# A four-part recurrence with eight experts behind it: expert 6's result by rows, paced index casts, a first slice in halves

## The chip, the core and the metric

The kernel runs on one core of one Trainium2 chip. A core has five engines that work at the same time, each with a queue of its own: TensorE (PE, products of matrices, with a separate row PEld for loading weights), VectorE (DVE), ScalarE (ACT), GpSimd (POOL) and SyncE (SP, which only issues transfers); GpSimd issues transfers too. They meet through semaphores. The metric is the device time of one execution in microseconds (us); less is better. The clock of TensorE has two levels, 1.2 and 2.4 GHz, and the profile shows the granted one as a share of the full clock.

## The reference, cut to what matters

```python
# attention: a recurrence over seq = 768 for 4 x 8 heads of 48
for t in range(S):
    S_re, S_im = ar*S_re - ai*S_im + kv, ar*S_im + ai*S_re      # a_re, a_im normalised by min(mag, .999)/(mag + 1e-6)
    y[:, :, t] = np.einsum('bhd,bhde->bhe', q[:, :, t], S_re)
# 3072 tokens of 384 -> the expert of the largest logit, in the order of tokens, up to a capacity
logits = x @ w_gate;  expert_idx = np.argmax(logits, axis=1);  gate_w = probs[arange(N), expert_idx]
disp[e, counts[e]] = x[i]                                        # 8 experts
h = np.maximum(np.einsum('ecd,edf->ecf', disp, w1), 0.0)         # 384 -> 1024
y = np.einsum('ecf,efd->ecd', h, w2)                             # 1024 -> 384
out[i] = gate_w[i] * y[expert_idx[i], pos[i]]
```

## The kernel before

Attention is done in four groups of eight units (a unit is one batch's chunk of 96 tokens). For each group, slices of the decay factors are loaded, normalised (`norm`: a square on ScalarE, then logarithm, exponential and three VectorE steps per slice, L305 to L374) and multiplied up by a scan (`scan`: pairs of VectorE steps, L404 and L409, that go through the slice from its last position to its first). The scaled queries and keys go through a scratch tensor in HBM (`scr`) and come back turned. A unit then has transposes and products on TensorE (`tr` L629, `pa` L645, `y` L706 and L711), a mask on VectorE (`a_sb`, L649), a copy to `xt` on ScalarE (L900), the gate's product (L924), a turn back to tokens (L911) and a last copy on ScalarE (L917), with which the unit's 96 rows of x are complete.

Behind groups of units comes a routing round (`routing`; the table `CUTS` says after which chunk of which group): logits (L952), the choice of the expert (L960 to L965), counts (`pp`, L970, L975), slots (L983 to L986), the weight (L996 to L1006), one cast of the slot numbers to an index per chunk of 96 tokens (L1010, VectorE), and one scatter for each chunk (`send`, L1024, GpSimd), which writes 96 rows of x to `disp`, the tensor of the experts' rows in HBM. Seven transfers first fill `disp` (L853). The last three chunks are `LATE`: expert 0's rows are read from `disp` (`mload`, L1074, SP's queue) when all other chunks have been sent, and the three chunks' rows are added to them on TensorE (`mt`: L1094 turns what was read, L1088 adds a chunk through a 0/1 matrix `own`, L1084).

The second stage goes through the experts in turn in steps of 128 of the 1024 hidden columns: the first product (`ph`, L1220, nine products), its split into two parts (ScalarE L1266, VectorE L1267), and the second product two steps later. For experts 0 to 6 that is `second` (L1228), with tokens on the columns of the result; at the expert's end the result is copied (L1166 to L1168), turned (`yt`, L1174), scaled (L1184, VectorE) and scattered to the output (L1185, GpSimd). The last expert has `second_rows` (L1241), with tokens on the partitions of the result, which needs no copy and no turn.

All of the attention stage is ordered by a planner (`Plan`): each operation has an engine, a cost written by hand and a due time (`want`), worked out from `BEGIN`, the planned start of each group; the planner picks the operation that can start first and writes the order of each engine's queue. `apart` sets a least distance between the planned starts of two operations, here between one send and the next (`APART`, one number for each group). `fill_gaps` then puts products that nobody reads (`s_all` from `ident`, L226) into gaps of TensorE's plan that are over 0.4 us, from a planned time `begin` on. The queues run in this order; the planned times are not kept on the chip.

Of the kernel before, what the change touches and what calls it, by code (L numbers as in the profile page):

```python
# [172 lines left out]
def dve(n):  # L173
    return .068 + n * .00104


def act(n):
    return .045 + n * .00086


class Att:
# [95 lines left out]

    def norm(self, g, j, s0):

        nc, plan = self.nc, self.plan  # L280
# [25 lines left out]
        o = plan.op(K + ("xa",), "ACT", act(2 * n * D) + .1, xa, w, after=[K + ("load",)], bufs=[a_, a4_])  # L306
        if g == 0 and j < 1:
            def xb():
                x = self.a4[g, j][:, 0:n, 3, :]
                nc.vector.tensor_tensor(out=x, in0=st['sq'][:, 0], in1=st['sq'][:, 1], op=ALU.add)  # L310
                st[0] = x
            o = plan.op(None, "DVE", dve(n * D), xb, w, after=[o], bufs=[a4_])
            parts = [(0, n, o, a4_)]
        elif by_dma:
            def acc():
                nc.gpsimd.dma_start(out=st['flat'][:, 0], in_=st['flat'][:, 1], accum_op=ALU.add)
            o = plan.op(K + ("acc",), "POOL", .6, acc, w - 2, after=[o], bufs=[a4_], kb=24 * n, extra=3.)
            parts = [(0, n, o, a4_)]
        else:
            parts = self.sums_of(plan, K, lambda: (st['sq'][:, 0], st['sq'][:, 1]), n, [o], w, st, [a4_])  # L320
# [60 lines left out]
    def scan(self, g, j, wants):  # L381
# [3 lines left out]
        n = SIZES[j]  # L385
        a4_ = ("a4", g, j)
        for s in range(n - 1, -1, -1):
            if j == 0 and s == n - 1:
# [23 lines left out]
            before = [("s", g) + prev[1:]] if ("s", g) + prev[1:] in plan.names else []  # L412
            m = plan.op(None, "DVE", .27, None, want, after=before + [K + ("i",), K + ("r",)], bufs=bufs)
            a = plan.op(("s", g, j, s), "DVE", .169, None, want, after=[m], bufs=[a4_, xy_])
# [315 lines left out]
    def routing(self, b, c, w, span):  # L730
# [18 lines left out]
        for i in range(n):  # L749
            x = plan.op(None, "DVE", .12, fs['cast'][i], w + (5 + i) * s, after=[o])  # L750
            o_ = plan.op(K(("send", i)), "POOL", 1.0, fs['send'][i], w + (5 + i) * s, after=[x] + ([("mload",)] if (b, c + 1) in LATE else []), kb=148, extra=2.)
            if rt.scattered is not None:
                o_.apart = (rt.scattered, APART[b])
            rt.scattered = o_

# [5 lines left out]
NACC = 4  # L761
BEGIN = (13, 67, 135, 203, 271)
FIRST = 8
BEHIND = 6
APART = (5, 5, 2.6, 1)

# [18 lines left out]

CUTS = [(0, 8), (1, 8), (2, 8), (3, 5), (3, 6), (3, 7), (3, 8)]
LATE = CUTS[-3:]
# [249 lines left out]
class Moe:  # L1037
# [119 lines left out]
    def finish_ops(self, e, tail, py):  # L1157
# [20 lines left out]
        def send(t):  # L1178
            m = parts[t]
            pt = py[t] if e == E_ - 1 else turn(t)  # L1180
            if 'o' not in st:
                st['o'] = self.p_x.tile([128, NT, DM], F32, tag="o", name=f"o_{e}", bufs=1)
            o = st['o']
            nc.vector.tensor_scalar(out=o[:m, t], in0=pt[:m, :DM], scalar1=tail[:m, t, 0:1], scalar2=None, op0=ALU.mult)  # L1184
            ins = nc.gpsimd.indirect_dma_start(  # L1185
                out=self.out, out_offset=bass.IndirectOffsetOnAxis(ap=tail[:m, t, 1:2].bitcast(U32), axis=0),
                in_=o[:m, t, :], in_offset=None, bounds_check=N - 1, oob_is_err=False).ins
            for other in self.scatters:
                self.tc.declare_no_dep(ins, other, reason="rows of different tokens")
            self.scatters.append(ins)  # L1190
        return [evac] + [lambda t=t: send(t) for t in range(len(parts))]

    def run(self, order, perm, check):
# [42 lines left out]
        def second_rows(e, f, hh, hl, py, t):  # L1236

            hi, lo = (w[1] for w in self.w[e, f // self.PF])
            ts, m = slice(t * LP, t * LP + LAST[t]), LAST[t]
            for i, (a, r) in enumerate(((hh, hi), (hl, hi), (hh, lo))):  # L1240
                nc.tensor.matmul(out=py[t][:m, :DM], lhsT=a[:, ts], rhs=r[:, f % self.PF],  # L1241
                                 start=f == 0 and i == 0, stop=f == NF - 1 and i == 2)
        py = {}
        LP, LAST = tiles(WIDTH[-1])
        c_order = ExitStack()
        c_order.enter_context(self.tc.manual_schedule(engines=ALL))
        for s in range(E_ * NF):
# [21 lines left out]
            if f == 0:  # L1269
                py[e] = [self.ps.tile([128, 512], F32, tag=f"y{m}", name=f"my{m}_{e}") for m in range(len(LAST) if e == E_ - 1 else KT)]  # L1270
            queue.append((e, f, hh, hl, py[e]))
            if len(queue) > self.LAG and s < E_ * NF - 1:
                x = queue.pop(0)
                if x[0] < E_ - 1:
                    second(*x)
                else:
                    for t in range(len(LAST)):
                        second_rows(*x, t)
            for op in later.pop(s, []):
                op()  # L1280
        assert not later
        fin = self.finish_ops(e, rows[e]['tail'], py[e])
        for t in range(len(LAST)):
            for x in queue:
                second_rows(*x, t)
            fin[1 + t]()
# [179 lines left out]
def kernel(ctx, tc, q, k, v, a_re, a_im, w_gate, w1, w2, av, xv, cen, vp, out):  # L1466
# [5 lines left out]
    with ExitStack() as c_main, ExitStack() as c_att:  # L1472
# [20 lines left out]
        for r in range(E_ * T // 512):  # L1493
            plan.op(("fill", r), "POOL", .9, lambda r=r: box['fill'][r](), 9 + 3 * r, kb=772)
        order = plan.solve()
        plan.fill_gaps(att.keep)
        cut = max(i for i, o in enumerate(order) if o.idx < early) + 1
# [118 lines left out]
```

## Time and profile before

| what | value |
|---|---|
| median of 3 runs | 640.82 us (640.61 to 641.45) |
| the profiled execution | 641.58 us, span 639.9 us, mean granted clock 0.936 |
| TensorE busy | 561.8 us (88%) |
| VectorE busy | 458.9 us (72%) |
| ScalarE busy | 383.5 us (60%) |
| GpSimd busy | 212.9 us (33%) |

Busy time is an average over stages with different limits, so the rows further down go by stages. The profiled execution has its own time: its span is the time between the first and the last instruction in the trace, and 1.7 us lie around it.

### The profile page before, as it was taken

The numbers are of one execution on the slowest core, as the hardware profiler recorded it, in microseconds if no ns is written. First come the engines' busy times: TensorE is split into PE (matmuls) and PEld (weight loads), VectorE is DVE, ScalarE is ACT, GpSimd is POOL, SyncE is SP. The second block draws the span as 40 slices with busy tenths as digits, with TensorE's granted clock in tenths as the row PEclk, the third lists the DMA queues.
The fourth block names the chain that finished last, engine by engine and source line by source line (L and its number), as shares of the span: only waits on it lengthen the run. The fifth ranks groups of instructions, "written<-read, shape, count | busy, mean of one in ns | idle before, by whom it ended". The sixth has DMA issues, their size and how long they took to land.

```text
span 639.9 us, 13273 instructions
## 1 busy us (share of the span) xinstructions
PE 561.8 (88%) x4662; PEld 489.7 (77%) x4662; DVE 458.9 (72%) x1340; ACT 383.5 (60%) x1034; POOL 212.9 (33%) x293
## 2 busy tenths in 40 slices
PE   2364569998999989999896889999999999999994
PEld 1122258786887868888785877999999999999993
DVE  3899979999999998999763244546665655655651
ACT  6465689989998899977652421344445344444540
POOL 9532314524459925464525031002020202112012
PEclk9666679999999999999999779999999999999997
DMA  6985588968899787885997231364545454455311
GB/s 214 297 245 147 147 203 231 241 189 207 196 230 251 213 228 168 213 223 135 215 242 209 55 91 29 109 184 125 163 129 158 138 169 155 155 165 159 101 37 37
DMA packets 75629, 108.81 MB, mean 170 GB/s; under 512 B 11716, under 2 KB 65853, under 8 KB 75553
## 3 DMA queue, kind: packets, MB, share of 16 engines
q1 hardware_dynamic: 58192, 57.37, 33.3%
q0 software_dynamic: 17360, 50.50, 29.1%
q8 instruction: 39, 0.64, 0.4%
q14 instruction: 38, 0.30, 0.2%
HBM read 71.51 MB, written 32.47 MB: 163 GB/s over the span
## 4 chain that ended last, share of the span: by engine, by line
PE 55%; DVE 20%; DMA 10%; ACT 9%; issue 4%; POOL 1%; POOLq 0%; DVEq 0%; ACTq 0%; SPq 0%
PE ph L1220 17%; PE my L1228 15%; DVE xy L404 4%; DMA scr<-qko 3%; DVE a L409 3%; PE pa L645 3%; PE tr L629 2%; DMA raw<-in_moe_w_dram 2%; PE n L272 2%; PE my L1241 2%; DMA qkc<-scr 2%; DVE qko L452 2%; PE s_all L660 2%; PE y L706 2%; DMA a<-in_av_dram 2%
## 5 line engine op out<-in xcount | busy, mean ns | idle before, releaser
L1266 ACT ACTIVATE hh<-ph 128x448 fp32r<-128x448 f32 (+7 forms) x64 | 32.7, 511 | 92.1 <-PE ph L1220 81.8
L1267 DVE SCALAR_TENSOR_TENSOR hl<-ph,hh 128x448 fp32r<-128x448 f32 (+7 forms) x64 | 37.2, 581 | 60.4 <-ACT hh L1266 59.6
L1185 POOL DMA_INDIRECT out_dram<-o,xr x26 | 25.7, 987 | 162.8 <-DVE o L1184 159.5
L1130 DVE TENSOR_TENSOR lo<-raw,hi 128x384 fp32r<-128x384 f32 (+2 forms) x128 | 65.7, 553 | 9.8 <-ACT hi L1129 9.7
L272 PE MATMUL n<-a,ident 128*128 128x384 f32 x92 | 44.8, 622 | 28.7 <-ACT a L305 28.7
L1220 PE MATMUL ph<-xh,hi 128*128 128x448 f32 (+7 forms) x192 | 69.5, 362 | 0.0
L1220 PE MATMUL ph<-xh,lo 128*128 128x448 f32 (+7 forms) x192 | 66.5, 347 | 0.0
L404 DVE TENSOR_TENSOR xy<-a 128x192 f32<-128x192 f32 (+1 forms) x199 | 61.5, 322 | 1.3 <-ACT a L374 1.1
L1129 ACT CAST hi<-raw 128x384 fp32r<-128x384 f32 (+2 forms) x128 | 59.1, 512 | 2.8 <-DMA raw<-in_moe_w_dram 2.8
L673 POOL DMA_DIRECT2D z<-sx x56 | 47.4, 1003 | 39.8 <-PE pa L645 12.4
L629 PE MATMUL tr<-ident,qkc 81*96 81x81 f32 x512 | 53.8, 241 | 5.6 <-DMA qkc<-scr 2.6
L1228 PE MATMUL my<-hh,lo 128*128 128x448 f32 (+6 forms) x168 | 58.7, 349 | 0.0
L1228 PE MATMUL my<-hh,hi 128*128 128x448 f32 (+6 forms) x168 | 58.6, 349 | 0.0
L1228 PE MATMUL my<-hl,hi 128*128 128x448 f32 (+6 forms) x168 | 58.6, 349 | 0.0
L649 DVE TENSOR_TENSOR a_sb<-pa,mask 96x384 f32<-96x384 f32 x64 | 35.1, 552 | 32.1 <-PE pa L645 21.1
L1024 POOL DMA_INDIRECT disp<-x,idx x32 | 42.1, 1315 | 46.1 <-DVE lm L961 22.4
L645 PE MATMUL pa<-qT,kT 128*96 128x96 f32 x512 | 56.9, 256 | 0.5 <-issue 0.4
L629 PEld LDWEIGHTS tr<-ident,qkc 81*96 81x96 f32 x512 | 43.3, 130 | 13.3 <-issue 4.0
L645 PEld LDWEIGHTS pa<-qT,kT 128*96 128x96 f32 x512 | 51.2, 170 | 2.5 <-issue 1.6
L272 PEld LDWEIGHTS n<-a,ident 128*128 128x128 f32 x92 | 20.0, 237 | 42.8 <-ACT a L305 24.6
L272 PE MATMUL p<-qko,ident 128*128 128x384 f32 x80 | 37.4, 598 | 15.3 <-ACT qko L441 15.2
L409 DVE TENSOR_TENSOR a<-xy 128x96 f32<-128x96 f32 (+1 forms) x218 | 49.8, 240 | 0.4
(224 smaller groups left out, 1459.0 us busy)
## 6 DMA issues: line engine op xcount, KB each, us to landing
raw<-in_moe_w_dram SPq DMA_DIRECT2D x64, 384.0 KB
qkc<-scr SPq DMA_DIRECT2D x32, 480.0 KB
scr<-qko POOLq DMA_DIRECT2D x44, 192.0 KB
scr<-qko POOLq DMA_DIRECT2D x20, 384.0 KB
a<-in_av_dram POOLq DMA_DIRECT2D x18, 384.0 KB
qkin<-in_xv_dram POOLq DMA_DIRECT2D x18, 384.0 KB
disp<-fill POOLq DMA_DIRECT2D x7, 772.0 KB
v<-in_vp_dram SPq DMA_DIRECT2D x32, 144.0 KB
```

The source lines that it names most:

```text
L272: nc.tensor.matmul(out=pt[:, :m], lhsT=self.ident, rhs=t[:, h:h + m], start=i == 0, stop=i == 1)
L404: nc.vector.tensor_tensor(out=st['xy'][:, :, cs].rearrange("p (u z) d -> p u z d", u=2), in0=a4[:, s, :, cs].rearrange("p (u z) d -> p u z ...
L409: nc.vector.tensor_tensor(out=self.a4[g, j][:, s, 0:2, cs], in0=xy[:, 0:4:2, cs], in1=xy[:, 1:4:2, cs], op=ALU.add)
L629: nc.tensor.transpose(out=pt[:, h * C:h * C + NE], in_=qk[:NE, 4 * hh + h, z_ * C:z_ * C + C], identity=self.ident[:NE, :NE])
L645: nc.tensor.matmul(out=pa[:, h * C:h * C + C], lhsT=kT[:, 4 * hh + h], rhs=qT[:, 4 * hh + h], start=True, stop=True)
L673: nc.gpsimd.dma_start(out=zn[a.start:a.stop or C], in_=st['sx'][o], accum_op=ALU.add)
L1024: ins = nc.gpsimd.indirect_dma_start(out=self.disp, out_offset=bass.IndirectOffsetOnAxis(ap=idx[:, c:c + 1], axis=0), in_=self.row(b, c0 + ...
L1129: return (lambda: nc.scalar.copy(out=hi[i][:, s], in_=raw[i][:, s]), lambda: nc.vector.tensor_tensor(out=lo[i][:, s], in0=raw[i][:, s], in ...
L1130: lambda: nc.vector.tensor_tensor(out=lo[i][:, s], in0=raw[i][:, s], in1=hi[i][:, s].bitcast(F32), op=ALU.subtract))
L1220: nc.tensor.matmul(out=ph[:, :W], lhsT=a[:, k, fs], rhs=r[:, k, :W], start=i == 0, stop=i == len(parts) - 1)
L1228: nc.tensor.matmul(out=py[m][:, :W], lhsT=a[:, f % self.PF, ms], rhs=r[:, :W], start=f == 0 and i == 0, stop=f == NF - 1 and i == 2)
L1267: nc.vector.scalar_tensor_tensor(out=hl[:, :W], in0=ph[:, :W], scalar=0.0, in1=hh[:, :W].bitcast(F32), op0=ALU.max, op1=ALU.subtract)
```

## The change

1. Expert 6, whose 384 rows fill three parts of 128, gets `second_rows` as the last expert has it. `BY_ROWS` is [6, 7]. Each part's scale and scatter follow its last product.
2. `apart` moves from the send to the index cast, with other distances.
3. `CUTS` gets (3, 4): one more routing round, for one chunk. `LATE` is still the last three.
4. The first slice is loaded and normalised in two halves of four positions (`norm_first`), and the scan starts when the later half is done.
5. `BEGIN` is 3 us earlier for all groups, and the seven fills of `disp` have planned times of their own (`FILL`).
6. `fill_gaps` begins at 58 us of the plan instead of 82.

```diff
+    def norm_first(self, s0):
+        n = SIZES[0]
...
+        for p, h in enumerate(range(n - HALF, -1, -HALF)):
+            i = slice(h, h + HALF)
...
+                nc.sync.dma_start(out=st['a'][:, :, i], in_=self.av[0][:, :, STARTS[0] + i.start:STARTS[0] + i.stop, :])
...
+            plan.op(K + ("i", p), "ACT", act(m) + .08 * (p == 0), ci, v + 7.5, after=[oi], bufs=[a4_])
+            plan.op(K + ("r", p), "ACT", act(m), cr, v + 7.5, after=[orr], bufs=[a4_])
...
             x = plan.op(None, "DVE", .12, fs['cast'][i], w + (5 + i) * s, after=[o])
-            o_ = plan.op(K(("send", i)), "POOL", 1.0, fs['send'][i], w + (5 + i) * s, after=[x] + ([("mload",)] if (b, c + 1) in LATE else []), kb=148, extra=2.)
+            plan.op(K(("send", i)), "POOL", 1.0, fs['send'][i], w + (5 + i) * s, after=[x] + ([("mload",)] if (b, c + 1) in LATE else []), kb=148, extra=2.)
             if rt.scattered is not None:
-                o_.apart = (rt.scattered, APART[b])
-            rt.scattered = o_
+                x.apart = (rt.scattered, APART[b])
+            rt.scattered = x
...
-BEGIN = (13, 67, 135, 203, 271)
+FILL = (9, 13, 17, 21, 43, 47, 62)
+HALF = 4
+BEGIN = (10, 64, 132, 200, 268)
...
-APART = (5, 5, 2.6, 1)
+APART = (5, 5, 2, 1.4)
...
-CUTS = [(0, 8), (1, 8), (2, 8), (3, 5), (3, 6), (3, 7), (3, 8)]
+BY_ROWS = [e for e, w in enumerate(WIDTH) if len(tiles(w)[1]) == KT]
+CUTS = [(0, 8), (1, 8), (2, 8), (3, 4), (3, 5), (3, 6), (3, 7), (3, 8)]
...
-            pt = py[t] if e == E_ - 1 else turn(t)
+            pt = py[t] if e in BY_ROWS else turn(t)
...
-                if x[0] < E_ - 1:
+                if x[0] in BY_ROWS:
+                    fin = self.finish_ops(x[0], rows[x[0]]['tail'], x[4]) if x[1] == NF - 1 else None
+                    for t in range(KT):
+                        second_rows(*x, t)
+                        if fin:
+                            fin[1 + t]()
+                else:
                     second(*x)
...
-            plan.op(("fill", r), "POOL", .9, lambda r=r: box['fill'][r](), 9 + 3 * r, kb=772)
+            plan.op(("fill", r), "POOL", .9, lambda r=r: box['fill'][r](), FILL[r], kb=772)
         order = plan.solve()
-        plan.fill_gaps(att.keep)
+        plan.fill_gaps(att.keep, begin=58.)
```

Where the planner now puts things is seen from the order of the queues. In VectorE's queue before, at the end of the routing round of group 2 (eight chunks, `idx_2_0`), between the masks `a_sb` of the following units:

```order
L1005 TENSOR_SCALAR ok_2_0_4836<-se_2_0_4835 96x8
L1006 TENSOR_REDUCE fine_132<-ok_2_0_4836 96x1
L1010 CAST idx_2_0_4844<-slot_2_0_4803 96x1 x3
L649 TENSOR_TENSOR a_sb1_123<-pa_3_6_0_4815,mask_272 96x384
L649 TENSOR_TENSOR a_sb1_123<-pa_3_6_1_4852,mask_272 96x384
L1010 CAST idx_2_0_4844<-slot_2_0_4803 96x1 x5
L649 TENSOR_TENSOR a_sb0_122<-pa_0_7_0_4920,mask_272 96x384
L649 TENSOR_TENSOR a_sb0_122<-pa_0_7_1_4942,mask_272 96x384
```

The same place in VectorE's queue of the changed kernel (L1101 is the cast, L737 the mask, L1051 to L1056 the choice of the next routing round, which has four chunks now):

```order
L1101 CAST idx_2_0_4908<-slot_2_0_4867 96x1
L737 TENSOR_TENSOR a_sb1_123<-pa_3_6_0_4879,mask_273 96x384
L737 TENSOR_TENSOR a_sb1_123<-pa_3_6_1_4916,mask_273 96x384
L1101 CAST idx_2_0_4908<-slot_2_0_4867 96x1 x2
L737 TENSOR_TENSOR a_sb0_122<-pa_0_7_0_4976,mask_273 96x384
L1101 CAST idx_2_0_4908<-slot_2_0_4867 96x1
L737 TENSOR_TENSOR a_sb0_122<-pa_0_7_1_5002,mask_273 96x384
L1051 TENSOR_REDUCE mx_3_0_5044<-lg_3_0_5024 96x4
L1052 TENSOR_TENSOR lm_3_0_5045<-lg_3_0_5024,mx_3_0_5044 96x32
L1054 SCALAR_TENSOR_TENSOR oh_3_0_5046<-lm_3_0_5045,dec_295 96x32
L1055 TENSOR_REDUCE first_3_0_5047<-oh_3_0_5046 96x4
L1101 CAST idx_2_0_4908<-slot_2_0_4867 96x1
```

Eight casts that stood in two blocks now stand one or two at a time among the masks and the next round's small steps; the remaining three follow further down in the same way, and those of the next two rounds too.

The end of attention in TensorE's queue before, from the last chunk's logits (`lg_3_7`) on:

```order
L911 MATMUL x_3_7_5328<-ident_60,xt_3_7_5313 96x128 x4
L952 MATMUL lg_3_7_5347<-sel_281,lt_3_4539 96x8
L226 MATMUL s_all_130<-ident_60 128x128 x11
L970 MATMUL pp_3_7_5378<-oh_3_7_5357,tri_286 96x8
L975 MATMUL pp_3_7_5378<-run_301,ones_289 96x8
L1094 MATMUL mt_0_0_5381<-ident_60,xr_0_4402 128x112 x4
L1088 MATMUL mt_0_0_5381<-own0_5262,x_3_4_5025 128x448
L1094 MATMUL mt_0_1_5399<-ident_60,xr_0_4402 128x112 x4
```

The same place after (L1043 is the logits, L1061 and L1066 the counts, L1185 and L1179 the turns and sums for expert 0's rows):

```order
L226 MATMUL s_all_130<-ident_60 128x128 x3
L1015 MATMUL y_3_7_5394<-xt_3_7_5431,wg_278 32x96 x4
L1002 MATMUL x_3_7_5441<-ident_60,xt_3_7_5431 96x128 x4
L1043 MATMUL lg_3_7_5449<-sel_282,lt_3_4633 96x8
L1185 MATMUL mt_0_0_5452<-ident_60,xr_0_4475 128x112 x4
L1179 MATMUL mt_0_0_5452<-own0_5368,x_3_4_5085 128x448
L1185 MATMUL mt_0_1_5475<-ident_60,xr_0_4475 128x112 x4
L1061 MATMUL pp_3_7_5480<-oh_3_7_5465,tri_287 96x8
L1066 MATMUL pp_3_7_5480<-run_302,ones_290 96x8
```

The eleven products that nobody reads are gone from behind the logits, three stand ahead of them, and the first turns of what `mload` read (`xr`) stand ahead of the counts. In the whole queue the number of such products goes from 51 to 89; 40 are in the planned stage 58 to 90 us.

## Rows read from the trace of the kernel before

**Rows 1.** Windows: busy us (instructions) by engine, then granted clock, DMA share, GB/s.

```profile
0.00:23.00 23.00, 7.89 (x13) 3.71 (x13) 10.88 (x34) 13.58 (x30) 20.00 (x59) 0.85 0.80 238
70.00:90.00 20.00, 11.26 (x35) 7.02 (x36) 17.05 (x51) 13.88 (x36) 6.29 (x9) 0.59 0.78 190
90.00:300.00 210.00, 201.83 (x2282) 168.61 (x2280) 202.40 (x619) 187.58 (x576) 110.43 (x129) 0.99 0.82 208
350.00:361.00 11.00, 7.39 (x71) 6.67 (x72) 1.11 (x2) 3.88 (x11) 1.55 (x2) 0.54 0.39 103
466.00:477.00 11.00, 11.00 (x68) 10.53 (x67) 7.09 (x20) 3.79 (x10) 4.01 (x4) 1.00 0.54 158
```

**Rows 2.** Timeline of ScalarE: start us, us, engine line op, [idle before <-releaser]; last copies of units.

```profile
340.89 0.48 ACT L917 COPY x<-x 96x384 f32<-96x384 f32 x1
...
355.28 0.48 ACT L917 COPY x<-x 96x384 f32<-96x384 f32 x1 [0.53 <-PE x L911]
...
362.56 0.47 ACT L917 COPY x<-x 96x384 f32<-96x384 f32 x1 [0.30 <-PE x L911]
...
368.08 0.48 ACT L917 COPY x<-x 96x384 f32<-96x384 f32 x1 [0.30 <-PE x L911]
...
380.79 0.47 ACT L917 COPY x<-x 96x384 f32<-96x384 f32 x1 [0.75 <-PE x L911]
...
386.73 0.48 ACT L917 COPY x<-x 96x384 f32<-96x384 f32 x1 [0.30 <-PE x L911]
```

**Rows 3.** Timeline of GpSimd, 339 to 385 us: scatters.

```profile
342.19 1.04 POOL L1024 DMA_INDIRECT disp<-x,idx  x1 [0.30 <-DVE a_sb L649]
...
350.93 0.92 POOL L1024 DMA_INDIRECT disp<-x,idx  x1 [0.30 <-issue]
370.44 0.93 POOL L1024 DMA_INDIRECT disp<-x,idx  x1 [18.58 <-DVE lm L961]
...
383.63 0.91 POOL L1024 DMA_INDIRECT disp<-x,idx  x1 [7.34 <-DVE oh L965]
```

**Rows 4.** Timeline of all engines, 351 to 353.5 us.

```profile
351.58 0.48 ACT L900 COPY xt<-y 128x384 f32<-128x384 f32 x1 [8.34 <-remote]
...
352.12 0.55 PE L924 MATMUL y<-xt,wg 128*32 128x96 f32 x8 [5.37 <-issue]
```

**Rows 5.** Chain that ended last: start us, us, what.

```profile
0.82 3.81 DMA a<-in_av_dram
...
8.91 0.57 DVE lnn L344
...
12.01 6.04 DMA a<-in_av_dram
...
74.45 2.93 PE n L272 x4
...
127.64 1.35 PE n L272 x4
```

**Rows 6.** Timeline of the head, 12 to 22.8 us.

```profile
13.04 0.43 DVE L404 TENSOR_TENSOR xy<-a 128x96 f32<-128x96 f32 x2 [1.12 <-ACT a L374]
...
16.24 1.68 POOL L853 DMA_DIRECT2D disp<-fill  x2
...
22.38 0.25 DVE L242 TENSOR_TENSOR mask<-ptok,tokrow 96x96 f32<-96x96 f32 x1 [2.33 <-ACT tokcol L241]
```

**Rows 7.** Timeline of TensorE, 386 to 400 us.

```profile
386.53 0.29 PE L952 MATMUL lg<-sel,lt 128*96 128x8 f32 x2
386.67 2.70 PE L226 MATMUL s_all<-ident 128*128 128x128 f32 x22
...
399.14 0.45 PE L1220 MATMUL ph<-xh,hi 128*128 128x448 f32 x1
```

**Rows 8.** Timeline of VectorE, first choice step of a one-chunk routing round.

```profile
370.09 0.16 DVE L960 TENSOR_REDUCE mx<-lg 96x1 f32<-96x8 f32 x1 [0.20 <-ACT lg L956]
```

**Rows 9.** Timeline of TensorE, behind expert 6's last product.

```profile
610.78 0.82 PE L1174 MATMUL yt<-ident,ys 128*128 128x128 f32 x6
```

More of the change, by code (lines that the diff above doesn't have):

```diff
@@ L280, in norm, with norm_slice @@
+    def norm_slice(self, g, j, s0):
         nc, plan = self.nc, self.plan
@@ L306, in norm @@
         o = plan.op(K + ("xa",), "ACT", act(2 * n * D) + .1, xa, w, after=[K + ("load",)], bufs=[a_, a4_])
[L307 to L314, printed above, removed]
+        if by_dma:
             def acc():
@@ L386, in scan, with ready @@
         a4_ = ("a4", g, j)
+        def ready(s):
+            p = ((n - 1 - s) // HALF,) if g == 0 and j == 0 else ()
+            return [K + ("i",) + p, K + ("r",) + p]
         for s in range(n - 1, -1, -1):
@@ L412, in scan @@
             before = [("s", g) + prev[1:]] if ("s", g) + prev[1:] in plan.names else []
-            m = plan.op(None, "DVE", .27, None, want, after=before + [K + ("i",), K + ("r",)], bufs=bufs)
+            m = plan.op(None, "DVE", .27, None, want, after=before + ready(s), bufs=bufs)
             a = plan.op(("s", g, j, s), "DVE", .169, None, want, after=[m], bufs=[a4_, xy_])
@@ L1238, in second_rows @@
             hi, lo = (w[1] for w in self.w[e, f // self.PF])
-            ts, m = slice(t * LP, t * LP + LAST[t]), LAST[t]
+            P, parts = tiles(WIDTH[e])
+            m = parts[t]
+            ts = slice(t * P, t * P + m)
             for i, (a, r) in enumerate(((hh, hi), (hl, hi), (hh, lo))):
@@ L1243, in run @@
         py = {}
-        LP, LAST = tiles(WIDTH[-1])
         c_order = ExitStack()
@@ L1269, in run @@
             if f == 0:
-                py[e] = [self.ps.tile([128, 512], F32, tag=f"y{m}", name=f"my{m}_{e}") for m in range(len(LAST) if e == E_ - 1 else KT)]
+                py[e] = [self.ps.tile([128, 512], F32, tag=f"y{m}", name=f"my{m}_{e}") for m in range(KT)]
             queue.append((e, f, hh, hl, py[e]))
@@ L1273, in run @@
                 x = queue.pop(0)
-                if x[0] < E_ - 1:
+                if x[0] in BY_ROWS:
[4 more added lines that the diff above has]
+                            fin[1 + t]()
+                else:
                     second(*x)
-                else:
-                    for t in range(len(LAST)):
-                        second_rows(*x, t)
             for op in later.pop(s, []):
@@ L1282, in run @@
         fin = self.finish_ops(e, rows[e]['tail'], py[e])
-        for t in range(len(LAST)):
+        for t in range(KT):
             for x in queue:
```

64 lines of the change are left out of this document (added).

## The prediction

> **What bounds the kernel now.** I read the busy time by stages first. In the attention stage from 90 to 300 us VectorE works 202.40 of 210 us, so there VectorE is the bound and what it loses earlier arrives at the end undiminished; in the first 23 us it works only 10.88, idle for 12.1 [rows 1]. From about 400 us the second stage (the eight experts) is TensorE without gaps, as the stretch 466 to 477 shows: 11.00 of 11 us at full clock [rows 1]. Between the two lies the tail of attention, 340 to 400 us, where no engine is busy: from 350 to 361 VectorE works 1.11 us and TensorE 7.39 at a granted clock of 0.54 (the lower of the two levels, 1.2 GHz) [rows 1]. So I read that tail unit by unit. ScalarE's last copy of a unit (L917) ends it; the starts of these copies are the unit times: 14.39, 7.28, 5.52, 12.71 and 5.94 us, together 45.84 from 340.89 to 386.73 [rows 2]. Two of five are undisturbed, mean 5.73; five of those would be 28.65. **17.2 us are excess**, and it sits in two units.
>
> Both lie over a block of scatters on GpSimd's queue: eight with starts 342.19 to 350.93, one each 1.25 us, and five from 370.44 on in the same rhythm [rows 3]. In the first block ScalarE's copy L900 starts at 351.58 after 8.34 us of idle time, released by something the trace calls remote, half a microsecond after the eighth scatter began, though its input left TensorE long before; TensorE then resumes at 352.12 after 5.37 us put down to issue [rows 4]. No operand is late there: the engines stand still until the block ends, and afterwards TensorE has the lower clock. That is my reading of the cause; what exactly the scatters hold up, the rows don't show.
>
> **Part 1, the casts are paced.** A scatter needs its index cast (L1010). Before, all casts of a route stand in two blocks in VectorE's order and release the sends together; now two or more rows of other work stand between most of them, so that eight sends spread over some two units instead of 9.7 us. What it returns: nothing at least (the scatters cost the same wherever they stand), 17.2 at most. The nearest row for scatters that are not in a block is the stretch 466 to 477, with four scatters in pairs on GpSimd and TensorE at 11.00 of 11 [rows 1]: no loss at all. But there TensorE had a long queue of ready products, and here a unit is a chain of small steps over four engines, and some casts still stand in twos. I take two thirds of the excess: **-11.4**.
>
> **Part 2, the first slice in halves.** The first scan step starts at 13.04 us, from 0.82 behind a 384 KB load (3.81) and a chain of eleven halvable steps [rows 5, 6]. A half-width VectorE step costs some 0.36 instead of 0.57 (estimate from 0.43 for two of 96 columns and 0.57 for 384 [rows 5, 6]: a fixed part stays), so 11 x 0.2 = 2.2, and the half load lands up to 1.9 earlier, say 1.2: the scan could start near 9.7. Behind it waits the mask (L242 at 22.38, idle 2.33), which needs GpSimd's constants, and these stand behind five fills of 0.84 each (the last two 16.24 to 17.92) [rows 6]; three of these move behind them, 2.5 us earlier. The second slice's load ends at 18.07 [rows 5] and is in a stretch with the DMA engines 0.80 busy [rows 1]; three fills of 772 KB fewer at 238 GB/s are 9.7 us of transfer out of its way. The extra instructions (six VectorE steps more, their fixed part about 0.15 each) lie in the 12.1 idle us. Bounds 0 and -5; I take **-2**.
>
> **Part 3, keep-alive products from 58 us.** Between 70 and 90 us the clock is 0.59 and VectorE idles for 2.95 [rows 1]; four turns of a slice take 2.93 us there (at 74.45, and once more in this stage) and 1.35 at 127.64 [rows 5]. Both back would be 3.2, but VectorE has only 2.95 idle and other waits in it. Bounds 0 and -2.95; with 40 more such products in that stage, in gaps of TensorE, I take **-1**.
>
> **Part 4, the order at the end.** Before, behind the last routing logits (386.53) come eleven keep-alive products and the counts, then twelve products that build expert 0's rows; the first expert product is at 399.14, 12.61 after [rows 7]. The keep-alives (2.70 at half clock) go, and the parts that don't need the last token chunk move ahead of the counts. What is left is 0.29, 9.4 of the twelve and the turns (389.50 to 399.14 less the overlap) and 0.45, some 10.4: **-2.2**, if VectorE's choice of the last chunk is ready in the meantime. Bounds -1 (TensorE waits for it) and -2.7.
>
> **Part 5, one more route.** Chunk (3,4) leaves the batch of five and is routed alone. It costs TensorE two more pairs of small products, 0.29 for one pair [rows 7], and VectorE 20 steps of 0.16, 3.2 us [rows 8]. VectorE is idle in most of the tail, so most is hidden; but these steps stand in its order before the cuts of a unit. Bounds 0 and +3.2: **+1.0**.
>
> **Part 6, expert 6's second product by rows.** Nine turns of its result go: six take 0.82, so nine 1.2, less what overlaps with the neighbours [rows 9]: **-1.0**. The products cost the same in either form. VectorE's three scales (L1184, 384 columns, so some 0.57 each by [rows 5]) now read the accumulators themselves, which expert 7 needs again one row of nine products after the last of expert 6, about 1.5 us; the first two can run while the third part's products do, and a copy of the same width went from VectorE there. Bounds -1.2 and +0.5, when the last scale holds the accumulator.
>
> **Where a page speaks against part 1.** ScalarE and TensorE stood still in the first block, for 8.34 and 5.37 us [rows 4]; that is what a cause outside the scatters would have to explain. The Trainium skill, "SBUF — State Buffer", section "Who interferes with whom", says that DMA never contends with a compute engine and that TensorE and ScalarE never wait on anyone: by that rule the block isn't the cause and the pacing returns nothing, and the time would be the 636 of rival C. The trace agrees only so far as the scatters in pairs at 466 go.
>
> **The sum.** Against the profiled execution's own 641.58: -11.4 -2 -1 -2.2 +1.0 -1.0 = -16.6, so 625.0; that execution lies 0.76 above the median of 640.82, where the same sum gives 624.2. I say **624.5**.
>
> **The rivals.**
> *B, half the block's stall stays.* The thirteen sends (now 8 + 4 + 1) still come within a few units, and each costs something wherever it is: 17.2 / 13 is 1.3 us a scatter. For it: the excess goes roughly with the number (8.66 + 1.55 over eight, 6.98 over five, 1.3 to 1.4 each). If half of that remains per scatter, part 1 gives -5: about 631.
> *C, the scatters are not the cause.* What is late at 351 is a transfer or code that would be late anyway; only the head, the end and expert 6 pay. 640.82 - 2 - 1 - 2.2 + 1.0 - 1.0, near 636. For it: "remote" names no scatter. Against it: it ends with the block both times.
> *D, slower, by one mechanism: the load of expert 0's rows comes too late.* It is issued after the last send that isn't late, now that of (3,4), and before it had landed by 383.3, when the next scatter, which waits for it, could go (383.63 after 7.34 idle) [rows 3]. TensorE needs it now right behind the last logits, where before the keep-alives and the counts stood, some 3 us. Counted to the end of those logits, 386.82 [rows 7], 3.5 us were to spare. If pacing makes the last send late by more than the tail gets shorter, TensorE waits. With the tail 11 us shorter and the send at its old place it would wait 7.5 and still gain; slower than 640.82 it becomes when the load lands 3.5 + 16.6 = 20 us later against the chain than before: then 643 to 648.
> *E, the change doesn't do what it says.* The casts stand apart in the order but VectorE is idle, so they may run as fast as before as soon as the route is done, wherever its neighbours aren't waiting. Then the block stays, and the time is C's.
>
> **How the numbers follow.** What a measurement can tell from no change here is about 0.2%, 1.3 us. A, most of the stall back (618 to 629): 0.55, the likeliest. B, 629 to 634: 0.20. C and E, 634 to 639: 0.13. Within 0.2% (head and end also give nothing): 0.05. D: 0.07. Faster by over 0.2%: 0.55 + 0.20 + 0.13 = 0.88, of which I move 0.03 to the middle since C's terms are small: 0.85; same 0.07; slower 0.08. The range leaves out the slower cases above and something below: from 616 (all of the excess and the head's bound, 640.82 - 17.2 - 5 - 1 - 2.2 + 1 - 1 is 615.4) to 638 (C with half its gains).
>
> **What would show it.** In the profile after: unit times (L917) of 5.5 to 7 us throughout, scatters more than 2 us apart, no 8 us of "remote" ahead of L900, and a clock near 1 in the tail (part 1 right; a block with spaced scatters and the same waits makes C right; waits of a microsecond behind each, B). First scan near 10 us (part 2); turns of slices at 1.35 in the stage around 75 us (part 3); from the last logits to the first expert product 10.4 us without a wait for the row load (part 4; a wait there is D); no gap ahead of expert 7's first product by rows (part 6). The number is wrong if the tail's stalls move to another load, or if VectorE, full up to 300 us, pays for the extra steps.

## The result and the profile after

The changed kernel takes **623.95 us** (median of 4 runs, 623.21 to 625.0), the kernel before beside it 640.98 (4 runs, 640.61 to 641.45): a ratio of **0.9735, 95% interval 0.9716 to 0.9754**, 17 us less. The forecast was 624.5. The profiled execution after took 623.21 with a span of 621.3, 18.6 less than the span before.

The windows of the changed kernel, in the first four stretches of [rows 1]:

```profile
0.00:23.00 23.00, 6.58 (x12) 3.23 (x13) 13.66 (x48) 15.45 (x40) 19.39 (x67) 0.83 0.62 197
70.00:90.00 20.00, 18.49 (x137) 15.49 (x136) 19.08 (x58) 17.18 (x46) 6.35 (x10) 0.91 0.87 229
90.00:300.00 210.00, 202.22 (x2322) 169.74 (x2319) 202.83 (x620) 188.44 (x576) 109.34 (x131) 0.99 0.82 209
350.00:361.00 11.00, 8.56 (x126) 7.75 (x126) 5.23 (x30) 4.28 (x14) 4.74 (x6) 1.00 0.24 69
```

In the head VectorE works 13.66 us instead of 10.88, between 70 and 90 us 19.08 instead of 17.05 at a granted clock of 0.91 instead of 0.59. Up to 300 us it remains the bound. From 350 to 361 TensorE has the full clock and VectorE 5.23 us of work instead of 1.11. The second stage, which lies earlier now, is as it was: from 452 to 463 us TensorE works 11.00 of 11 us at full clock.

The timeline of ScalarE in the tail, with the last copy of each of the last six units (L1008, which was L917) and two of the copies L991 (which was L900; L733, which their waits name, was L645):

```profile
336.67 0.48 ACT L1008 COPY x<-x 96x384 f32<-96x384 f32 x1
...
341.94 0.48 ACT L991 COPY xt<-y 128x384 f32<-128x384 f32 x1 [3.17 <-PE pa L733]
...
343.48 0.48 ACT L1008 COPY x<-x 96x384 f32<-96x384 f32 x1
...
348.42 0.47 ACT L1008 COPY x<-x 96x384 f32<-96x384 f32 x1
...
357.29 0.48 ACT L991 COPY xt<-y 128x384 f32<-128x384 f32 x1 [4.04 <-PE pa L733]
...
359.19 0.48 ACT L1008 COPY x<-x 96x384 f32<-96x384 f32 x1
...
364.98 0.47 ACT L1008 COPY x<-x 96x384 f32<-96x384 f32 x1 [1.27 <-PE pa L733]
...
371.42 0.48 ACT L1008 COPY x<-x 96x384 f32<-96x384 f32 x1 [0.30 <-PE x L1002]
```

The five last units take 6.81, 4.94, 10.77, 5.79 and 6.44 us, together 34.75, where [rows 2] had 45.84. Two copies L991 still wait over 3 us. The scatters of GpSimd that stand around those two places:

```profile
337.47 1.02 POOL L1115 DMA_INDIRECT disp<-x,idx  x1 [2.17 <-DVE idx L1101]
...
340.30 0.92 POOL L1115 DMA_INDIRECT disp<-x,idx  x1 [0.30 <-issue]
...
353.58 0.92 POOL L1115 DMA_INDIRECT disp<-x,idx  x1 [2.04 <-DVE sl L1074]
...
356.26 0.92 POOL L1115 DMA_INDIRECT disp<-x,idx  x1 [0.33 <-issue]
```

Three scatters start from 337.47 to 340.30 and three from 353.58 to 356.26, 1.3 to 1.6 us apart; the two long copies' waits end 1.64 and 1.03 us after the last of each three has started. Over the thirteen scatters from 337.47 to 363.34, six of the twelve distances are still under 2 us.

The head, VectorE's timeline (the answer to [rows 6]):

```profile
9.48 0.36 DVE L492 TENSOR_TENSOR xy<-a 128x192 f32<-128x192 f32 x1 [0.23 <-ACT a L353]
...
17.30 0.25 DVE L242 TENSOR_TENSOR mask<-ptok,tokrow 96x96 f32<-96x96 f32 x1 [1.56 <-ACT tokcol L241]
```

The first scan step starts at 9.48 instead of 13.04, the mask at 17.30 instead of 22.38. The end of attention on TensorE (the answer to [rows 7]):

```profile
371.21 0.28 PE L1043 MATMUL lg<-sel,lt 128*96 128x8 f32 x2
371.36 1.12 PE L1185 MATMUL mt<-ident,xr 112*128 112x112 f32 x8
...
381.36 0.45 PE L1311 MATMUL ph<-xh,hi 128*128 128x448 f32 x1
```

From the last logits to the first expert product 10.15 us pass instead of 12.61, without a wait. And behind expert 6's last product on TensorE (the answer to [rows 9]) the next product follows at once, no turn between them:

```profile
589.56 0.34 PE L1334 MATMUL my<-lo,hh 128*128 128x384 f32 x1
589.74 0.33 PE L1311 MATMUL ph<-xh,hi 128*128 128x372 f32 x1
```

So in this pair of traces the 18.6 us come apart into the prediction's own parts. All units ahead of the tail end 4.22 earlier (336.67 for 340.89), the five units of the tail take 11.09 less, the way from the last logits to the first expert product 2.46 less, and the rest of the program 0.82 less (621.3 - 381.36 against 639.9 - 399.14).

### The profile page after: what moved, and what is told of

Its sections match the earlier page's. It is cut to its first block, busy times and chain, and to the rows that moved or that the text cites. A ratio compares the mean times of both kernels' runs of the same rounds, so it can differ in the third digit from the quotient of the medians.

```text
span 621.3 us, 13468 instructions
## 1 busy us (share of the span) xinstructions
PE 557.6 (90%) x4731; PEld 490.3 (79%) x4731; DVE 461.9 (74%) x1365; ACT 383.3 (62%) x1043; POOL 209.3 (34%) x293
## 4 chain that ended last, share of the span: by engine, by line
PE 53%; DVE 18%; ACT 16%; DMA 5%; POOL 4%; issue 3%; POOLq 0%; another core or an unknown queue 0%; ACTq 0%; SPq 0%; DVEq 0%
PE ph L1311 17%; PE my L1319 13%; PE my L1334 4%; DVE xy L492 4%; ACT z L768 3%; PE pa L733 3%; DVE a L497 3%; PE tr L717 2%; DMA scr<-qko 2%; ACT ends L615 2%; DVE qko L540 2%; PE y L794 1%; PE yt L1265 1%; PE mt L1242 1%; DVE qko L575 1%
## 5 line engine op out<-in xcount | busy, mean ns | idle before, releaser
L733 PE MATMUL pa<-qT,kT 128*96 128x96 f32 x512 | 55.2, 252 | 0.7 <-ACT kT L721 0.7
L272 PE MATMUL n<-a,ident 128*128 128x384 f32 x92 | 40.7, 574 | 16.3 <-ACT a L396 16.3
L1115 POOL DMA_INDIRECT disp<-x,idx x32 | 39.5, 1233 | 39.4 <-ACT lt L1018 9.2
L733 PEld LDWEIGHTS pa<-qT,kT 128*96 128x96 f32 x512 | 49.8, 166 | 2.9 <-ACT kT L721 1.1
L1319 PE MATMUL my<-hh,lo 128*128 128x448 f32 (+5 forms) x144 | 50.6, 351 | 0.0
L1319 PE MATMUL my<-hh,hi 128*128 128x448 f32 (+5 forms) x144 | 50.6, 351 | 0.0
L1319 PE MATMUL my<-hl,hi 128*128 128x448 f32 (+5 forms) x144 | 50.5, 351 | 0.0
L737 DVE TENSOR_TENSOR a_sb<-pa,mask 96x384 f32<-96x384 f32 x64 | 35.1, 549 | 16.9 <-PE pa L733 12.8
L1311 PE MATMUL ph<-xl,hi 128*128 128x448 f32 (+7 forms) x192 | 45.8, 346 | 0.0
```

The lines of the kernel that those rows point to most:

```text
L272: nc.tensor.matmul(out=pt[:, :m], lhsT=self.ident, rhs=t[:, h:h + m], start=i == 0, stop=i == 1)
L733: nc.tensor.matmul(out=pa[:, h * C:h * C + C], lhsT=kT[:, 4 * hh + h], rhs=qT[:, 4 * hh + h], start=True, stop=True)
L1115: ins = nc.gpsimd.indirect_dma_start(out=self.disp, out_offset=bass.IndirectOffsetOnAxis(ap=idx[:, c:c + 1], axis=0), in_=self.row(b, c0 + ...
L1311: nc.tensor.matmul(out=ph[:, :W], lhsT=a[:, k, fs], rhs=r[:, k, :W], start=i == 0, stop=i == len(parts) - 1)
L1319: nc.tensor.matmul(out=py[m][:, :W], lhsT=a[:, f % self.PF, ms], rhs=r[:, :W], start=f == 0 and i == 0, stop=f == NF - 1 and i == 2)
```

## The experiments

They ran on three chips, and on each of them the kernel before took 625.4 to 625.9 us (13 to 17 runs, 622.6 to 631.1), not 641; on which chip the first pair ran is not on record. That is the first finding, and the kernels below are to be read beside it; medians and ratios are always those to the kernel before on the same chip. Where single traces are compared, mind their spread: the first of the last six units ends (L917) at 340.51 to 342.61 in four traces with the same order of instructions up to there (the kernel before twice, the second and the third experiment).

| kernel | median us | ratio to before, 95% interval |
|---|---|---|
| changed kernel, second and third time | 617.85, 617.12 | 0.987 (0.9838 to 0.9902), 0.9863 (0.9828 to 0.9898) |
| before, casts paced alone | 624.59 | 0.9977 (0.995 to 1.0005) |
| changed, casts in blocks | 618.91 | 0.9875 (0.9817 to 0.9934) |
| before, first slice in halves, BEGIN and FILL alone | 626.1 | 1.0016 (0.9994 to 1.0039) |
| changed, keep-alive products from 82 us | 622.41 | 0.9947 (0.9918 to 0.9975) |
| changed, without the extra cut | 619.7 | 0.9905 (0.9869 to 0.9941) |
| changed, expert 6 as before | 619.99 | 0.9912 (0.9882 to 0.9942) |
| changed, no extra cut, blocks, no idle products at the end | 623.31 | 0.9958 (0.9933 to 0.9984) |
| before, profiled again | 627.12 (one run) | |
| before without eight scatters | 624.17 (one run) | |
| before with eight scatters 3.7 us apart | 638.51 (one run) | |

**1. The pacing alone.** In the kernel before:

```diff
-                o_.apart = (rt.scattered, APART[b])
-            rt.scattered = o_
+                x.apart = (rt.scattered, APART[b])
+            rt.scattered = x
...
-APART = (5, 5, 2.6, 1)
+APART = (5, 5, 2, 1.4)
```

> The kernel before with only the paced index casts (least distance on the cast, 2 and 1.4 us for groups 2 and 3). Theory T (blocks of scatters stall the engines): of the 17.2 us of excess in the five last units 9 to 12 return, so 629 to 632. Theory C (the blocks are not the cause; the gain of the change in the tail comes from its other parts): within 2 us of 641.

It took 624.59 where the kernel before took 625.77: nothing clear of the measurement. The edit did spread the scatters: the eight start from 342.07 to 355.68, over 13.6 us instead of 8.7, and the last five units take 28.56 us. Theory T's 629 to 632 and theory C's 641 were both made for a kernel that takes 641.

**2. The scatters apart by work on GpSimd.** All queues as before, except (`pad` is the part of the fill buffer that holds zeros anyway):

```diff
...
             idx = st['idx']
+            if b == 2:
+                for _ in range(5):
+                    nc.gpsimd.memset(self.pad, 0.0)
             ins = nc.gpsimd.indirect_dma_start(
```

> The kernel before, every engine's order kept, but with five fills of a buffer (0.43 us each) on GpSimd ahead of each of the eight scatters of group 2, so that they start 3.4 us apart instead of 1.25. Theory T: the 8.34 us wait ahead of the copy L900 falls under 3 us, and the unit of 14.39 us under 9; since the block now reaches to about 369, part of it returns as short waits: 631 to 638. Theory C: the wait stays where it is, 641. A third, T2 (any long work on GpSimd stalls the others): the waits spread over 27 us, 645 to 660.

Measured: 638.51, just above T's range, but for another reason. The units are those of a kernel without any stall (340.51 to 369.12, 28.61 for five). What costs is the end, seen in GpSimd's first and last scatter of the eight and TensorE's queue behind the last logits:

```profile
344.26 1.04 POOL L1028 DMA_INDIRECT disp<-x,idx  x1 [0.47 <-issue]
...
370.21 0.92 POOL L1028 DMA_INDIRECT disp<-x,idx  x1 [0.43 <-DVE idx L1011]
```

```profile
368.92 0.28 PE L953 MATMUL lg<-sel,lt 128*96 128x8 f32 x2
...
383.50 2.02 PE L1098 MATMUL mt<-ident,xr 112*128 112x112 f32 x8 [11.47 <-DMA xr<-disp]
...
395.71 0.45 PE L1224 MATMUL ph<-xh,hi 128*128 128x448 f32 x1
```

The eight scatters start 3.7 us apart, so the following ones end later, and with them the load of expert 0's rows: TensorE waits for it 11.47 us, and its first turns then run at half the speed (2.02 for eight instead of 1.12). The first expert product starts 26.79 after the last logits. This is rival D's mechanism, and it costs 12.7 us against the kernel before. A total close to the range of a theory says little until the trace shows where it comes from.

**3. No scatters of group 2 at all.**

```diff
         def send(c):
+            if b == 2:
+                return
```

> The kernel before without the eight scatters of group 2 (their 768 tokens don't reach the experts' rows, all else is kept). Theory T: the unit of 14.39 us takes 5.5 to 7 and the clock stays high, 8.7 to 10.2 us less: 630 to 633. Theory C: what is late at 351 us is late without them too, 640 to 642.

It took 624.17, and the last copies of the units show the tail without the eight scatters (their tokens are missing from the result):

```profile
340.57 0.47 ACT L917 COPY x<-x 96x384 f32<-96x384 f32 x1
...
369.18 0.48 ACT L917 COPY x<-x 96x384 f32<-96x384 f32 x1 [0.30 <-PE x L911]
```

28.61 us for the five units, the same to 0.01 as with scatters 3.7 us apart.

**4. The changed kernel with casts in blocks**, the edit of the first experiment undone.

> The changed kernel with the distance back on the sends and its old values, so that the casts stand in blocks of 3, 5 and 4 again; all other parts kept. Theory T: 8 to 12 us of the tail are lost again, 632 to 636. Theory C: within 2 us of the changed kernel, 622 to 626.

It took 618.91, as the changed kernel does on that chip (617.85). Its scatters and its units:

```profile
337.99 1.01 POOL L1115 DMA_INDIRECT disp<-x,idx  x1 [0.76 <-DVE idx L1101]
...
346.92 0.92 POOL L1115 DMA_INDIRECT disp<-x,idx  x1 [0.30 <-ACT lm L1069]
```

```profile
337.17 0.47 ACT L1008 COPY x<-x 96x384 f32<-96x384 f32 x1
...
343.01 0.47 ACT L1008 COPY x<-x 96x384 f32<-96x384 f32 x1 [0.30 <-PE x L1002]
...
347.92 0.47 ACT L1008 COPY x<-x 96x384 f32<-96x384 f32 x1 [0.30 <-PE x L1002]
```

Eight scatters in a row, 1.22 to 1.56 us apart, lie over the units of 5.84 and 4.91 us; ScalarE's longest wait there is 1.49 us, for TensorE's products. So a block of scatters alone does not hold the engines: theory T fails in that form, and what is left of it is a block together with something that this chip did not have.

**5. The kernel before, profiled again**, without an edit.

> The kernel before, as it is, profiled again beside its own runs. Theory S (the stall of the tail is not a property of the order of scatters but of the chip or the hour in which the first trace was taken): if this chip gives about 625 us, ScalarE's copy L900 no longer waits 8 us for something remote, the five last units take 5 to 8 us each (29 to 31 in all instead of 45.84), and the scatters still start 1.22 us apart. If it gives 641, the stall lies over the block again, and theory T (the block itself) is alive. Theory T where the time is 625: the scatters must stand further apart than 1.22 us.

Its single run took 627.12. ScalarE's copies, and the first and the last of the eight scatters:

```profile
342.61 0.47 ACT L917 COPY x<-x 96x384 f32<-96x384 f32 x1
...
346.25 0.48 ACT L900 COPY xt<-y 128x384 f32<-128x384 f32 x1 [1.29 <-PE y L711]
...
371.23 0.48 ACT L917 COPY x<-x 96x384 f32<-96x384 f32 x1 [0.30 <-PE x L911]
```

```profile
343.86 1.04 POOL L1024 DMA_INDIRECT disp<-x,idx  x1 [0.30 <-DVE a_sb L649]
...
352.60 0.92 POOL L1024 DMA_INDIRECT disp<-x,idx  x1 [0.30 <-ACT qT L621]
```

The scatters stand exactly as in [rows 3], 1.25 us apart. But the copy L900 has waited 1.29 us, for TensorE's products and for nothing remote, where [rows 4] showed 8.34, and the five units take 28.62 us, where [rows 2] showed 45.84. The 17.2 us of excess are gone with the order of the instructions unchanged. The spans differ by 14.5 (639.9 and 625.4), since this execution is 1.72 later ahead of the tail (342.61 for 340.89) and needs 1.06 more from the last logits to the first expert product (13.67 for 12.61). Theory S holds.

The two traces side by side also show what was late in the first one. The load of v (L610, SyncE) and the copy L900 both wait for TensorE's products of one unit (L706, L711). In the first trace those products have ended by 344.42 in the record, the load follows at 349.36 and the copy at 351.58 [rows 4]; in the second they end at 346.15, and the load starts at 346.02 and the copy at 346.25:

```profile
344.09 0.33 PE L711 MATMUL y<-qT,z 128*48 128x96 f32 x4
...
349.36 0.33 SPq L610 DMA_DIRECT2D v<-in_vp_dram  x1
```

```profile
345.81 0.34 PE L711 MATMUL y<-qT,z 128*48 128x96 f32 x4
346.02 0.33 SPq L610 DMA_DIRECT2D v<-in_vp_dram  x1
```

So in the first trace two engines got the signal of the same products 4.9 and 7.2 us after their recorded end; the profile knows no sender close in time and writes "remote". Whether the products ended that much later than recorded (the ends of matmuls are modelled) or only their signal was late, and why, the trace does not tell.

**6. The changed kernel again**, on the same chip and later on another.

> The changed kernel as it is. Where the kernel before takes about 626: theory S says that the tail's 11 us are not to be had and what is left is the head (4), the end (2.4) and expert 6 (0.8), 617 to 620, a ratio of 0.987; theory T with a cost per scatter says that paced scatters still gain, 612 to 615. Where the kernel before takes 641: 622 to 626.

> The changed kernel beside a_best on the same chip. Where the kernel before takes about 626: 617 to 619, a ratio of 0.987; where it takes 641: 623 to 625.

617.85 and 617.12: 0.987 and 0.9863 of the kernel before, 8.0 and 8.7 us. Both as theory S expected. Against the trace of the kernel before on that chip the units end 3.42 earlier at the last logits (367.61 for 371.03), 3.05 come from there to the first expert product (10.62 for 13.67), and 1.23 behind it. TensorE's rows at the end, of the kernel before and of the changed one, both from this chip:

```profile
371.03 0.28 PE L952 MATMUL lg<-sel,lt 128*96 128x8 f32 x2
...
375.06 1.12 PE L1094 MATMUL mt<-ident,xr 112*128 112x112 f32 x8 [0.93 <-DMA xr<-disp]
...
384.70 0.45 PE L1220 MATMUL ph<-xh,hi 128*128 128x448 f32 x1
```

```profile
367.61 0.28 PE L1043 MATMUL lg<-sel,lt 128*96 128x8 f32 x2
368.24 1.12 PE L1185 MATMUL mt<-ident,xr 112*128 112x112 f32 x8 [0.34 <-DMA xr<-disp]
...
378.23 0.45 PE L1311 MATMUL ph<-xh,hi 128*128 128x448 f32 x1
```

Both wait for the load of expert 0's rows, 0.93 and 0.34 us. Without the stall TensorE's start on the experts hangs on this load in both orders.

**7. The head alone.** The changed kernel with the casts' pacing, the extra cut, the earlier keep-alive products (the products that nobody reads, L226) and expert 6's rows undone:

```diff
...
-BY_ROWS = [e for e, w in enumerate(WIDTH) if len(tiles(w)[1]) == KT]
-CUTS = [(0, 8), (1, 8), (2, 8), (3, 4), (3, 5), (3, 6), (3, 7), (3, 8)]
+BY_ROWS = [E_ - 1]
+CUTS = [(0, 8), (1, 8), (2, 8), (3, 5), (3, 6), (3, 7), (3, 8)]
...
-        plan.fill_gaps(att.keep, begin=58.)
+        plan.fill_gaps(att.keep)
```

> The kernel before with the first slice in halves and the new BEGIN and FILL alone (casts in blocks, old cuts, keep-alive products from 82 us, expert 6 as before). By the prediction's part 2: 2 us less than the kernel before, bounds 0 and 5; by the trace of the changed kernel, whose units before the tail were 4.2 us ahead with part 3 in it: 2.5 to 4 less. A rival: without the keep-alive products the gain is lost between 70 and 90 us, 0 to 1.

1.0016 of the kernel before: no gain that can be measured. The head itself does what it should: the first unit's last copy starts at 95.20, 3.8 ahead of the kernel before (99.02). But the lead does not last. The first of the last six units ends (L1008) at 341.02, inside the 340.51 to 342.61 of the order before, and the last logits stand at 369.43, where the second, the third and the fifth experiment have 368.92 to 371.03. From 312 to 341 us VectorE works only 16.54 of 29 us there, so it no longer sets the pace.

**8. The keep-alive products from 82 us.** `plan.fill_gaps(att.keep)` in place of `begin=58.` in the changed kernel.

> The changed kernel with the keep-alive products from 82 us of the plan instead of 58. Theory P (they give the attention its gain, by the clock between 70 and 90 us): the granted clock there falls from 0.91 to about 0.6, turns of slices take 2.93 us again, units end 2 to 4 us later, 0.991 to 0.994 of the kernel before. Theory H (the head gives it, as the prediction had for two thirds): 0 to 1 us, 0.987 to 0.989.

0.9947 against 0.987, 4.6 us by the medians, on different chips and with runs between 619.21 and 625.65. One window:

```profile
70.00:90.00 20.00, 12.29 (x60) 7.98 (x60) 17.66 (x53) 15.28 (x40) 5.17 (x8) 0.76 0.88 230
```

The clock between 70 and 90 us falls to 0.76 and four turns take 2.93 us again (at 73.14 in the chain), yet at 256 us its units are only 0.6 behind the changed kernel's (256.61 for 256.01), and at the last logits 2.58 (370.19 for 367.61). Most of that arises between 311 and 331 us, where ScalarE waits 6.3 us for a weight transfer and the following unit with it (4.8 in the changed kernel's trace). Theory H is out. Theory P's size fits (2 to 4 us in the units; its 0.991 to 0.994 meets the interval), but not its reason: the clock between 70 and 90 us carries only 0.6 of it in this trace. Why the weights land later is open.

**9. Without the extra cut.** `CUTS` as before in the changed kernel.

> The changed kernel without the extra cut (3,4), with its paced casts. The prediction had the extra route cost 1.0 and the new order behind the last logits give 2.2, as two parts. Theory K (the order at the end comes from the extra cut, since with five chunks in one round the planner puts the eleven idle products and the counts back behind the last logits): from the last logits to the first expert product 13.6 us again instead of 10.6, the whole kernel 2 to 3.5 us slower than the changed one where both are measured beside the same kernel before (0.991 to 0.993 of it, if the changed kernel stands at 0.987). The prediction's own: 1 us faster than the changed kernel, 0.985 or 0.986. If the kernel before takes 641 here: theory T says that five casts paced as before keep the tail short, within 2 us of 624 plus K's 3.

0.9905, close to theory K; the prediction's own 0.985 or 0.986 lies outside the interval. The trace tells more. TensorE behind the last logits:

```profile
364.13 0.28 PE L1043 MATMUL lg<-sel,lt 128*96 128x8 f32 x2
364.27 2.70 PE L226 MATMUL s_all<-ident 128*128 128x128 f32 x22
...
368.12 1.12 PE L1185 MATMUL mt<-ident,xr 112*128 112x112 f32 x8
...
377.75 0.45 PE L1311 MATMUL ph<-xh,hi 128*128 128x448 f32 x1
```

The idle products are back and 13.62 us pass to the first expert product: theory K is right on the order. But the last logits come at 364.13, 3.48 ahead of the changed kernel's, so the first expert product starts 0.48 earlier. Not all of the 3.48 is the route's: 2.21 lie ahead of the last six units (335.78 for 337.99), where other traces of the changed order have 336.62 to 337.19, and 1.27 in the five units (28.55 for 29.82). So the extra route costs 1.3 in the units and gives 3.0 behind them; the sum, a gain of some 1.7, fits the medians (617.85 for 619.7), though they come from different chips and their intervals overlap.

**10. Expert 6 as before** in the changed kernel (`BY_ROWS = [E_ - 1]`).

> The changed kernel with expert 6's second product as before (copies and nine turns again): 0.8 to 1.0 us more than the changed kernel, all of it behind 590 us (part 6). A rival: the turns are hidden and the time is the same within 0.3.

619.99 against 617.85 on the same chip. From the first expert product to the end of the span it takes 240.62 (617.3 - 376.68), the changed kernel 239.47 (617.7 - 378.23): 1.15. The medians' 2.14 is more than that and not part 6's alone, if it is real: the intervals of the two ratios overlap.

**11. A version meant to beat both.** The changed kernel without the extra cut, with blocks of casts so that the load of expert 0's rows goes out early, and without idle products (the same L226) behind the last unit:

```diff
...
-APART = (5, 5, 2, 1.4)
+APART = (5, 5, .5, .2)
...
-                if end > begin and gap > least:
+                if begin < end < until and gap > least:
```

> The changed kernel without the extra cut, with its casts in blocks (least distance 0.5 and 0.2 us, so 1, 1, 6 and 5 together) so that the load of expert 0's rows goes out early, and without idle products behind the last chunk's copy; the planner then puts the first turns right behind the last logits. Theory S (blocks cost nothing where the kernel before takes about 626): last logits near 364 as without the extra cut, 10.1 to 10.6 us from there to the first expert product, 613 to 616, a ratio of 0.980 to 0.984. Theory K2 (the load's landing is what the end waits for in any order): no better than the changed kernel, 617 to 619. Theory T, where the kernel before takes 641: 628 to 634, slower than the changed kernel there.

It took 623.31, **slower than the changed kernel** (617.12 beside it). TensorE:

```profile
363.72 0.29 PE L1043 MATMUL lg<-sel,lt 128*96 128x8 f32 x2
367.11 2.02 PE L1185 MATMUL mt<-ident,xr 112*128 112x112 f32 x8 [3.11 <-DMA xr<-disp]
...
381.58 0.45 PE L1311 MATMUL ph<-xh,hi 128*128 128x448 f32 x1
```

The last logits are early (363.72), but the load, issued at 361.51, holds TensorE until 367.11, after 3.11 idle us. The granted clock is 0.50 from 367 to 375 us, and eight turns take 2.02 instead of 1.12. 17.86 us pass to the first expert product, where the changed kernel beside it needs 10.51 (366.82 to 377.33). The ninth experiment, with the idle products in that place, has neither the wait nor the slow turns (1.12): the products that I had priced as 2.70 us to be saved cover the wait and keep the clock up. Theory K2 was nearer, and it too left out the clock.

## Why the prediction was right

The number holds, and so do the sizes of its terms in the pair that it was made for. The reason of the largest term does not:

- **Part 1, pacing: -11.4 forecast, 12.3 less excess in the pair; that pacing took it away is not shown.** The excess of the tail was 17.22 before (45.84 against the undisturbed 28.62 of the fifth experiment, my estimate from two units was 28.65) and is 4.93 after (34.75 against 29.82 in the changed kernel's undisturbed trace, 337.99 to 367.81). Two thirds was a guess that no row priced, and 0.71 came: the largest term is right by luck.

  **The reason that I gave for the excess was wrong.** I wrote that no operand is late and that the engines stand still until the block ends. But TensorE's product at 352.12 reads the xt that ScalarE's copy at 351.58 writes [rows 4], so it waited for its operand; and that copy, like the load of v, waited for a signal of TensorE's products that came 4.9 to 7.2 us after their recorded end (fifth experiment).

  The block of scatters is no cause of its own: the same block holds nobody in the later traces, pacing alone gives nothing there (624.59 for 625.77), undoing it costs nothing that can be measured (618.91 for 617.85), and without the scatters the five units take the same 28.61. What the first pair had besides, chip or hour, no run shows; none of the experiments met it again. Whether pacing took the 12.3 away there is therefore argued, from the waits that are left over the two groups of three scatters in the changed kernel's trace; that another part of the change did it is not ruled out.

  Rival C, to which I gave the page's rule that DMA never contends with a compute engine (the Trainium skill, "SBUF — State Buffer", "Who interferes with whom"), was nearer to the cause than its chance said: the undisturbed traces agree with that rule, the first pair's 8.34 us wait stays unexplained by it.
- **Parts 2 and 3, head and keep-alive products: -3 forecast, -4.2 measured** at the first unit of the tail. The first scan step came to 9.48 where I had put 9.7, and the turns at 74.31 take 1.31 us (2.93 before). The split was off, and so was the premise that what VectorE loses early arrives at the end undiminished: the head alone is 3.8 ahead at the first unit and gives nothing that can be timed, since its lead is gone by 341 us (seventh experiment). The gain that lasts comes with the keep-alive products, 2.6 at the last logits, of which the clock between 70 and 90 us shows 0.6.
- **Part 4, the order at the end: -2.2 forecast, -2.46 measured**, and -3.05 in the pair of traces of the sixth experiment. The eleven idle products that go did not run at half clock, as I had it: the granted clock over them is 1.00. And my three terms (0.29, 9.4 and 0.45) add up to 10.1, not 10.4; 10.15 came. I treated this as a part of its own. It comes from the extra cut.
- **Part 5, the extra route: +1.0 forecast, +1.2 measured** (29.82 against 28.62 for five units), and 1.27 when the cut alone is undone. So parts 4 and 5 are one edit, which loses about 1.3 in the units and gains 3.0 behind them; by the medians it gains some 2 us, with intervals that overlap.
- **Part 6, expert 6: -1.0 forecast, -0.82 measured**, 1.15 behind the first expert product when it alone is undone. No wait ahead of expert 7's products.

Rival D, the late load, was the right danger. It did not decide, but without the stall both kernels wait for this load (0.93 and 0.34 us), and with the lower clock behind the wait it turned the second and the eleventh experiment into losses of 13 and 6 us. Rival B's price of a fixed sum for each scatter does not hold in the undisturbed traces, where eight scatters cost nothing. Rival E came half true: six of the twelve distances between the scatters stayed under 2 us.

What the change is worth depends on the machine's condition: 17 us (2.65%) in the first pair, 8 to 9 (1.3 to 1.4%) on the two chips where it was measured again and the kernel before takes 625.8 to 625.9 us. Against such a kernel the 16.6 us that the prediction adds up would have been twice too much.

## What to carry to other kernels

A wait whose releaser the trace cannot name, on several engines at once, is not yet a property of the kernel: profile the kernel a second time, on another chip, before a plan is built on it. Undo each part alone before it is credited with a term, since a cost and a gain that stand in different places can be one edit. And idle products in a wait are free until the wait is gone: what they cover, a transfer's landing and the clock, is to be looked up before they are removed. And when the profile writes "remote", look at what the waiting instruction reads and who else waited for the same sender.

## What was not expected of the hardware

- The same instructions in the same order took 641 us in one set of runs (640.61 to 641.45) and 625.8 on three chips (medians 625.37 to 625.87), and in the one trace of it with the short time five units of the tail take 17.2 us less (28.62 for 45.84), without ScalarE's waits for something remote, the longest of which was 8.34.
- In the first trace a load on SyncE and a copy on ScalarE started 4.9 and 7.2 us after the recorded end of the products that they wait for, in the second 0.1 us or less.
- TensorE after an idle 3.11 us ran eight turns in 2.02 us instead of 1.12, and after 11.47 us the same 2.02, at a granted clock of 0.50: the lower of the two levels. With idle products in that place it took 1.12.
- A scatter of 96 rows starts every 1.22 us when GpSimd has nothing else to do; eight in a row cost the other engines nothing in the undisturbed traces.
